# Second mixture: row loads released two experts ahead, transposes placed by a later landing, and token rows straight from the second layer for the last three experts

## Chip, cores and metric

The kernel runs on one core of one Trainium2 chip. The metric is the device time in microseconds (us); the profile also gives the span from the first to the last instruction of one execution.

## What is computed

A network of three parts, all in float32, with 1152 tokens of width 512:

```python
scores = q @ k.T / sqrt(64)                 # attention, 2 x 8 heads, 576 tokens, only the 32 largest of a row kept
x = softmax(masked scores) @ v              # 1152 x 512
P = sinkhorn(exp(x @ w_gate))               # mixture one: every token through all 8 experts
x = sum over e of P[:, e] * (relu(x @ w1[e]) @ w2[e])
expert = argmax(x @ w_gate2)                # mixture two: each token through one expert, at most 288 tokens each
out[i] = gate_w[i] * (relu(x[i] @ w1[expert]) @ w2[expert])      # w1: 512 x 1024, w2: 1024 x 512
```

Products are made in three float32r matmuls each (high x high, high x low, low x high), so each weight block and each activation is split into a high and a low part: ScalarE copies the high part, VectorE or GpSimd subtracts.

## The kernel before

**The order.** Nothing is issued in the order of the source. `job(engine, rank, cost, fn, deps, take, use, lag, more)` files a piece of work; `Order.run` is a planner that plays a clock for each engine, starts the job that can start first (the lowest rank among those that can start within 0.02 us) and writes its instructions into that engine's stream. Each engine then runs its own stream strictly in order. Dependencies given in `deps` act only in the plan; on the chip an instruction waits for the data and the buffers that it touches. A load on the SP queue is planned to have landed `lag + 2.3 + more` after its start or later, and what needs it is put into its engine's stream no sooner than that.

**Mixture two** (`mixture_two`) takes the experts in the order of their token counts, r = 0 to 7. From the code, expert r gets n = min(288, 1152/r) row slots, as S groups of P rows: r = 0 to 4 have 3 x 96, r = 5 has 2 x 116, r = 6 has 2 x 96, r = 7 has 2 x 82. For each expert:

- `gather` (L906): SP loads the expert's token rows from `disp` in DRAM into one of four row buffers (`x2`; two of them are halves of `xl`, which mixture one no longer needs), P partitions by S rows of 514 floats (512 values, the token's number, its gate weight).
- `ji` (L909): VectorE converts the token numbers to integers for the later scatter.
- `turn` (L918): TensorE transposes the rows, S transposes for each of 4 column blocks d; ScalarE (L922) and VectorE (L924) split the result into `hl` (printed as `v`). For r = 0 the columns come from another place.
- eight units f = 0 to 7: two weight blocks are loaded (L670, `ra` for layer 1, `rb` for layer 2, 3 buffers each) and split (`w0h`/`w0l` and `w1h`/`w1l` at L672 and L675; 3 and 4 pairs). Layer 1 (L939) is 12 matmuls of n columns; L686 and L688 apply the relu and split (`hh`, `hl`). Layer 2 (L951) has the weights stationary, 12 matmuls of n columns into 4 PSUM tiles `y`, which hold the output transposed.
- at the end 4 evictions (L959, L961) into `yt` (printed `yy`), 4 x S transposes back (`turn`, L967), S scalings by the gate weight (L974, L976) and S indirect scatters into `out` on GpSimd (L980).

TensorE's stream holds layer 1 of unit k+1 ahead of layer 2 of unit k. The ranks put the transposes of expert r beside units 1 to 4 of the expert before. Layer 1's output, `y`, and `hp` share 5 PSUM tiles (`psm`), given out in the order in which they are asked for: with four in `y`, one is left for layer 1.

Before the change, the load of expert r (r > 1) is released in the plan by the first layer-1 unit of expert r-1 (`begun`).

Of the kernel before, what the change touches and what calls it, by code (L numbers as in the profile page):

```python
# [162 lines left out]
def t_act(n, sbuf=False, ptr=0):  # L163
    return 0.05 + n * 0.000833 + 0.06 * sbuf + 0.09 * ptr


def t_dve(n, two=False):
    return 0.06 + n * 0.00104 + 0.08 * two
# [6 lines left out]
def t_pe(n):  # L175
    return max(0.109, n * 0.000443 + 0.0015)


class Net:
# [695 lines left out]
    def mixture_two(self):  # L875
        nc, E, DM, cap = self.nc, self.E, self.DM, self.cap
        fb = self.F // 128
        self.x2, self.i2, self.xs, self.yt, self.ob = (Pool([]) for _ in range(5))
        self.route_all()
        back, begun = [], None  # L880

        def over():
            self.xs.free += [(self.o.t["X"], x) for x in self.over]
            old = self.xt[1].rearrange("p a b -> p (a b)").bitcast(F32)
            self.x2.free += [(self.o.t["X"], old[:, i * 1542:(i + 1) * 1542].rearrange("p (s c) -> p s c", s=3))
                             for i in range(2)]
        self.job("X", 0, 0.0, over, deps=list(self.chain.values()))
        for r in range(E):
            n = min(cap, self.N // max(r, 1))
            S = -(-n // 128)  # L890
            P = -(-n // (2 * S)) * 2
            n = S * P
            x, idx, hl = self.x2.box(), self.i2.box(), self.xs.box()
            if r == 0:
                e, known = (lambda: slice(0, 1)), []
                row = lambda n=n: slice(0, n)
            else:
                e = lambda r=r: bass.ds(self.expert[r], 1)
                row = lambda r=r, n=n: bass.ds(self.expert[r] * cap, n)

                def read(r=r):
                    self.expert[r] = nc.sync.value_load(self.order_[0:1, r:r + 1], min_val=1, max_val=E - 1)
                known = [self.job("SP", -12, 0.1, read, deps=[self.sorted_])]

            def gather(x=x, row=row, P=P, S=S):
                nc.sync.dma_start(x.t[:P, :S], self.disp[row(), :].rearrange("(s p) d -> p s d", p=P))  # L906
            j = self.job("SP", -10 + 0.1 * r, 0.5, gather, deps=self.sent + [self.gate, begun if r > 1 else None] + known, take=[x],
                         lag=2.0, more=1.0)
            ji = self.job("DVE", 200 + r, 0.1, lambda x=x, idx=idx, P=P, S=S: nc.vector.tensor_copy(  # L909
                idx.t[:P, :S], x.t[:P, :S, 512]), deps=[j], take=[idx])  # L910
            turned = []
            for d in range(4):
                if r == 0:
                    p, jt = self.rows[d]
                else:
                    p = self.psa.box()

                    def turn(d=d, p=p, x=x, P=P, S=S):  # L918
                        for s in range(S):
                            self.tr(p.t[:, s * P:(s + 1) * P], x.t[:P, s, d * 128:(d + 1) * 128])  # L920
                    jt = self.job("PE", 1000 + self.unit + 13 + d, 0.11 * S, turn, deps=[j], take=[p], use=[x])
                jh = self.job("ACT", -950, t_act(n), lambda d=d, p=p, hl=hl, n=n: nc.scalar.activation(  # L922
                    hl.t[0][:, d, :n], p.t[:, :n], AF.Copy), deps=[jt], take=[hl] if d == 0 else [], use=[p, hl])
                jl = self.job("DVE", -950, t_dve(n), lambda d=d, p=p, hl=hl, n=n: nc.vector.tensor_sub(  # L924
                    hl.t[1][:, d, :n], p.t[:, :n], hl.t[0][:, d, :n].bitcast(F32)), deps=[jh], use=[p])
                turned += [jh, jl]
            y, hp, chain = [], [], {}
            yt, evicted = self.yt.box(), []
            for f in range(fb):
                k, rank = self.unit, 1000 + self.unit + 20  # L930
                self.unit += 1
                w1, w2 = self.weights(k, self.w21, self.w22, e, f, late=True, deps=known)
                while len(hp) < min(f + 2, fb):
                    hp.append(self.psm.box())
                h, p, j = self.h.box(), hp[f], None
                for m, (i, s, dep) in enumerate(((0, 0, w1[1]), (0, 1, w1[1]), (1, 0, w1[2]))):
                    def layer1(i=i, s=s, m=m, p=p, w1=w1, hl=hl, n=n):
                        for d in range(4):
                            nc.tensor.matmul(p.t[:, :n], w1[0].t[i][:, d, :], hl.t[s][:, d, :n],  # L939
                                             start=m == 0 and d == 0, stop=m == 2 and d == 3)  # L940
                    j = self.job("PE", rank - 1.5, 4 * t_pe(n), layer1, deps=turned + [dep, j],
                                 take=[p] if m == 0 else [], use=[w1[0], hl])
                begun = begun if f else j
                ready = self.parts(k, h, p, 0, n, [j], [h])
                for a in range(4):
                    if f == 0:
                        y.append(self.psm.box())

                    def layer2(a=a, f=f, h=h, w2=w2, y=y, n=n):
                        for m, (i, s) in enumerate(((0, 0), (0, 1), (1, 0))):  # L950
                            nc.tensor.matmul(y[a].t[:, :n], w2[0].t[s][:, a * 128:(a + 1) * 128], h.t[i][:, :n],  # L951
                                             start=f == 0 and m == 0, stop=f == fb - 1 and m == 2)
                    j = self.job("PE", rank, 3 * t_pe(n), layer2, deps=ready + [w2[1], w2[2], chain.get(a)],
                                 take=[y[a]] if f == 0 else [], use=[h, w2[0]])
                    chain[a] = j
                    if f == fb - 1:
                        def evict(a=a, y=y, yt=yt, n=n):
                            if a % 2:
                                nc.vector.tensor_copy(yt.t[:, a, :n], y[a].t[:, :n])  # L959
                            else:  # L960
                                nc.scalar.activation(yt.t[:, a, :n], y[a].t[:, :n], AF.Copy)  # L961
                        evicted.append(self.job("DVE" if a % 2 else "ACT", -940, t_dve(n), evict, deps=[j],
                                                take=[yt] if a == 0 else [], use=[y[a], yt]))
            for s in range(S):
                p, o = self.psa.box(), self.ob.box()

                def turn(s=s, p=p, yt=yt, P=P):  # L967
                    for a in range(4):
                        self.tr(p.t[:P, a * 128:(a + 1) * 128], yt.t[:, a, s * P:(s + 1) * P])
                j = self.job("PE", 1000 + self.unit + 21.6, 0.45, turn, deps=evicted, take=[p], use=[yt])  # L970

                def scale(s=s, p=p, o=o, x=x, P=P):
                    if s == 1:
                        nc.vector.tensor_scalar(o.t[:P], p.t[:P], x.t[:P, s, 513:514], None, op0=OP.mult)  # L974
                    else:
                        nc.scalar.activation(o.t[:P], p.t[:P], AF.Copy, scale=x.t[:P, s, 513:514])  # L976
                j = self.job("DVE" if s == 1 else "ACT", -100, 0.65, scale, deps=[j], take=[o], use=[p, x])

                def send(s=s, o=o, idx=idx, P=P):
                    i = nc.gpsimd.indirect_dma_start(  # L980
                        out=self.out, out_offset=bass.IndirectOffsetOnAxis(ap=idx.t[:P, s:s + 1], axis=0),
                        in_=o.t[:P], in_offset=None, bounds_check=self.N - 1, oob_is_err=False)
                    for x in self.outs:
                        self.tc.declare_no_dep(i.ins, x.ins, reason="other rows")
                    self.outs.append(i)
                back.append(self.job("POOL", 0, 1.0, send, deps=[j, ji] + self.zeroed, use=[o, idx], lag=3.0))
# [209 lines left out]
```

## Time and profile before

| | us |
|---|---|
| median of 3 runs (1314.46 to 1314.94) | 1314.78 |
| time of the profiled execution | 1314.3 |
| its span | 1312.5 |
| TensorE busy in it | 1260.8 (96%) |
| mixture two in it | about 1080 to 1312.5 |

"A <- B" in a row is "A is written from B". PE is TensorE's matmuls, ACT ScalarE, DVE VectorE, POOL GpSimd, SPq the queue that issues loads. "128*116 128x512" is a stationary operand of 128 by 116 and a moving one of 128 by 512. A wait is put down to what came last. Numbers are microseconds unless marked ns; `PEclk` is TensorE's granted clock as a share of full speed.

### The profile page before, as it was taken

To read this page: it belongs to the slowest core of one execution; us is meant where nothing else is said; L and a number is where in the kernel's file an instruction comes from. 1 tells how busy PE (TensorE), PEld (TensorE's weight loads), DVE (VectorE), ACT (ScalarE), POOL (GpSimd) and SP (SyncE) were. 2 spreads that over 40 slices of the span, in tenths; PEclk is the share of its full clock that TensorE was granted. 3 is DMA by queue.
4 is the path that set the end of the run, shared out by engine and by line. 5 is a ranking of instruction groups with operands and counts; after the bars stand their busy time and mean duration, and the time that the engine had idled before them with its cause. 6 is when DMAs were issued, how large, how long until landed. Compare 5 with 4: busy or idle time off the path is not lost.

```text
span 1312.5 us, 22337 instructions
## 1 busy us (share of the span) xinstructions
PE 1260.8 (96%) x7244; PEld 1085.8 (83%) x7244; DVE 963.5 (73%) x2333; ACT 765.4 (58%) x1787; POOL 363.9 (28%) x380
## 2 busy tenths in 40 slices
PE   7777999999999999999999999999999999999997
PEld 3434899988888888878888898999999979999996
DVE  7999999999999999955366676455555746665653
ACT  6857898888787777643433354444334524554643
POOL 5634677877444444430000010000000000011101
PEclk8999999999999999999999999999999999999989
DMA  4561465665233423234555465444444616665652
GB/s 113 141 225 33 118 172 164 180 181 160 86 105 102 123 76 101 67 106 127 170 171 170 136 197 170 127 124 126 128 128 122 192 34 181 198 181 169 189 166 53
DMA packets 228231, 180.90 MB, mean 138 GB/s; under 512 B 45060, under 2 KB 180228, under 8 KB 228114
## 3 DMA queue, kind: packets, MB, share of 16 engines
q1 hardware_dynamic: 224482, 174.58, 45.8%
q0 software_dynamic: 3024, 4.74, 1.1%
q8 instruction: 57, 0.93, 0.3%
q14 instruction: 60, 0.49, 0.1%
q10 hardware_dynamic: 608, 0.15, 0.1%
HBM read 159.20 MB, written 22.01 MB: 138 GB/s over the span
## 4 chain that ended last, share of the span: by engine, by line
PE 83%; DVE 7%; issue 3%; ACT 3%; DMA 2%; SPq 1%; POOL 0%; POOLq 0%; ACTq 0%; DVEq 0%
PE yp L752 30%; PE yp L728 30%; PE yp L939 5%; PE yp L951 5%; PE tp L222 5%; PE tp L621 3%; PE tp L514 3%; DVE wk L533 2%; DVE m L535 2%; DMA xl<-disp 1%; DMA x<-disp 1%; PE tp L1088 1%; DVE e L544 1%; ACT tp L542 1%; SPq L466 0%
## 5 line engine op out<-in xcount | busy, mean ns | idle before, releaser
L686 ACT ACTIVATE hh<-yp 128x256 fp32r<-128x256 f32 (+6 forms) x248 | 114.6, 462 | 241.3 <-PE yp L728 177.2
L672 ACT ACTIVATE w1h<-rb 128x512 fp32r<-128x512 f32 x248 | 156.6, 632 | 152.1 <-PE yp L752 116.3
L688 DVE SCALAR_TENSOR_TENSOR hl<-yp,hh 128x256 fp32r<-128x256 f32 (+6 forms) x248 | 128.3, 518 | 152.9 <-ACT hh L686 152.0
L752 PE MATMUL yp<-w1h,hh 128*128 128x512 f32 x552 | 223.1, 404 | 0.0
L752 PE MATMUL yp<-w1h,hl 128*128 128x512 f32 x552 | 217.0, 393 | 0.0
L752 PE MATMUL yp<-w1l,hh 128*128 128x512 f32 x552 | 216.9, 393 | 0.0
L675 DVE TENSOR_TENSOR w1l<-rb,w1h 128x512 fp32r<-128x512 f32 x160 | 110.6, 692 | 103.2 <-ACT w1h L672 102.8
L728 PE MATMUL yp<-xl,w0h 128*128 128x256 f32 (+2 forms) x768 | 167.1, 339 | 0.0
L728 PE MATMUL yp<-xh,w0h 128*128 128x256 f32 (+2 forms) x768 | 167.0, 339 | 0.0
L728 PE MATMUL yp<-xh,w0l 128*128 128x256 f32 (+2 forms) x768 | 166.9, 339 | 0.0
L672 ACT ACTIVATE w0h<-ra 128x512 fp32r<-128x512 f32 x256 | 159.9, 624 | 2.6 <-DMA ra<-in_moe_w_dram 2.6
L535 DVE MAX8 m<-wk 128x8 f32<-128x576 f32 x216 | 158.5, 744 | 0.5
L728 PEld LDWEIGHTS yp<-xh,w0h 128*128 128x128 f32 x768 | 131.3, 188 | 19.5 <-issue 0.4
L678 POOL TENSOR_TENSOR w0l<-ra,w0h 128x512 fp32r<-128x512 f32 x88 | 113.8, 1294 | 108.1 <-ACT w0h L672 103.6
L1147 POOL DMA_INDIRECT disp<-acc,idx x9 | 9.7, 1082 | 477.0 <-DVE run L1143 477.0
L728 PEld LDWEIGHTS yp<-xl,w0h 128*128 128x128 f32 x768 | 128.3, 189 | 9.5 <-issue 0.6
L728 PEld LDWEIGHTS yp<-xh,w0l 128*128 128x128 f32 x768 | 127.0, 189 | 9.4 <-issue 0.2
L678 POOL TENSOR_TENSOR w1l<-rb,w1h 128x512 fp32r<-128x512 f32 x88 | 113.9, 1294 | 61.0 <-ACT w1h L672 60.2
L752 PEld LDWEIGHTS yp<-w1h,hl 128*128 128x128 f32 x552 | 103.6, 188 | 22.7
L675 DVE TENSOR_TENSOR w0l<-ra,w0h 128x512 fp32r<-128x512 f32 x168 | 115.7, 689 | 6.2 <-ACT w0h L672 2.5
L752 PEld LDWEIGHTS yp<-w1h,hh 128*128 128x128 f32 x552 | 104.0, 188 | 17.1 <-issue 0.4
L752 PEld LDWEIGHTS yp<-w1l,hh 128*128 128x128 f32 x552 | 104.1, 189 | 14.3
(193 smaller groups left out, 2342.6 us busy)
## 6 DMA issues: line engine op xcount, KB each, us to landing
ra<-in_moe_w_dram SPq DMA_DIRECT2D x256, 256.0 KB, 2.8
rb<-in_moe_w_dram SPq DMA_DIRECT2D x256, 256.0 KB, 2.8
y<-ys SPq DMA_DIRECT2D x30, 256.0 KB, 2.1
ys<-y SPq DMA_DIRECT2D x22, 256.0 KB, 3.0
disp<-z SPq DMA_DIRECT2D x1, 4626.0 KB
qg<-in_q_dram SPq DMA_DIRECT2D x64, 64.0 KB, 2.3
vr<-in_v_dram SPq DMA_DIRECT2D x32, 128.0 KB, 2.3
yt<-y SPq DMA_DIRECT2D x10, 256.0 KB, 2.7
```

Source lines behind the costliest of these rows:

```text
L222: self.nc.tensor.transpose(out, in_, self.ident[:p, :p])
L514: nc.tensor.matmul(ps.t[:, :288], w, keys[k][0].t[:, half * 288:(half + 1) * 288], start=m == 0, stop=m == len(terms) - 1)
L535: j = self.job("DVE", r, 0.66, lambda i=i: nc.vector.max(m.t[:, i + 1], wk.t), deps=[j], use=[wk] if i == 2 else [])
L672: jh = self.job("ACT", -500 + rank, t_act(512, True), lambda r=r, w=w: nc.scalar.activation(w.t[0], r.t, AF.Copy), deps=[j], take=[w])
L675: jl = self.job("DVE", -100 + rank, t_dve(512, True), lambda r=r, w=w: nc.vector.tensor_sub(w.t[1], r.t, w.t[0].bitcast(F32)), deps=[jh], ...
L678: jl = self.job("POOL", -100 + rank, t_pool(512), lambda r=r, w=w: nc.gpsimd.tensor_sub(w.t[1], r.t, w.t[0].bitcast(F32)), deps=[jh], use=[r])
L686: jh = self.job("ACT", -1000 + k * 0.001, t_act(b - a), lambda: nc.scalar.activation(h.t[0][:, a:b], p.t[:, :b - a], AF.Relu), deps=deps, ...
L688: jl = self.job("DVE", -1000 + k * 0.001, t_dve(b - a), lambda: nc.vector.scalar_tensor_tensor(h.t[1][:, a:b], p.t[:, :b - a], 0.0, h.t[0] ...
L728: nc.tensor.matmul(p.t[:, :b - a], w1[0].t[i][:, d, :], self.xt[s][:, d, c0 + a:c0 + b], start=m == 0 and d == 0, stop=m == 2 and d == 3)
L752: nc.tensor.matmul(y[t].t, h.t[i][:, c:c + 128], w2[0].t[s], start=f == 0 and m == 0, stop=f == last and m == 2)
L939: nc.tensor.matmul(p.t[:, :n], w1[0].t[i][:, d, :], hl.t[s][:, d, :n], start=m == 0 and d == 0, stop=m == 2 and d == 3)
L951: nc.tensor.matmul(y[a].t[:, :n], w2[0].t[s][:, a * 128:(a + 1) * 128], h.t[i][:, :n], start=f == 0 and m == 0, stop=f == fb - 1 and m == 2)
```

## The change

Three edits in `mixture_two`:

1. `begun` becomes a list with one entry per expert, its layer 1 of unit f = 4; the load of expert r is released by entry r-2, that is some twelve units ahead of its own first unit where it was about eight.
2. The load's `more` goes from 1.0 to 6.5: the plan takes it as landed 5.5 us later, and puts the transposes and the number conversion later in their streams.
3. Where S is 2 (r = 5, 6, 7, `byrow`), layer 2 has the activations stationary (128 x P) and the weights moving (128 x 512): 6 matmuls of 512 columns a unit in place of 12 of n, into S PSUM tiles that hold token rows. The four evictions and the transposes back are gone; the scaling reads PSUM directly.

```diff
-        back, begun = [], None
+        back, begun = [], []
...
-            j = self.job("SP", -10 + 0.1 * r, 0.5, gather, deps=self.sent + [self.gate, begun if r > 1 else None] + known, take=[x],
-                         lag=2.0, more=1.0)
+            j = self.job("SP", -10 + 0.1 * r, 0.5, gather, deps=self.sent + [self.gate, begun[r - 2] if r > 1 else None] + known, take=[x],
+                         lag=2.0, more=6.5)
...
-            yt, evicted = self.yt.box(), []
+            byrow = S <= 2
+            yt, evicted = None if byrow else self.yt.box(), []
...
-                begun = begun if f else j
+                begun += [j] if f == 4 else []
                 ready = self.parts(k, h, p, 0, n, [j], [h])
-                for a in range(4):
+                for s in range(S if byrow else 0):
+                    if f == 0:
+                        y.append(self.psm.box())
+
+                    def rows2(s=s, f=f, h=h, w2=w2, y=y, P=P):
+                        for m, (i, t) in enumerate(((0, 0), (0, 1), (1, 0))):
+                            nc.tensor.matmul(y[s].t[:P], h.t[i][:, s * P:(s + 1) * P], w2[0].t[t],
+                                             start=f == 0 and m == 0, stop=f == fb - 1 and m == 2)
+                    chain[s] = self.job("PE", rank, 3 * t_pe(DM), rows2, deps=ready + [w2[1], w2[2], chain.get(s)],
+                                        take=[y[s]] if f == 0 else [], use=[h, w2[0]])
+                for a in range(0 if byrow else 4):
...
-                p, o = self.psa.box(), self.ob.box()
+                p, o = y[s] if byrow else self.psa.box(), self.ob.box()
...
-                j = self.job("PE", 1000 + self.unit + 21.6, 0.45, turn, deps=evicted, take=[p], use=[yt])
+                j = chain[s] if byrow else self.job("PE", 1000 + self.unit + 21.6, 0.45, turn, deps=evicted, take=[p], use=[yt])
```

## Rows read from the trace of the kernel before

**Rows 1.** The page, the chain that ended last, shares of the span by line.
```profile
PE yp L752 30%; PE yp L728 30%; PE yp L939 5%; PE yp L951 5%; PE tp L222 5%; PE tp L621 3%; PE tp L514 3%; DVE wk L533 2%; DVE m L535 2%; DMA xl<-disp 1%; DMA x<-disp 1%; PE tp L1088 1%; DVE e L544 1%; ACT tp L542 1%; SPq L466 0%
```

**Rows 2.** TensorE's waits, 1080 to 1312.5 us: total, times, longest.
```profile
PE tp L222 <- DMA xl<-disp: 3.5, 2, 2.0
PE tp L222 <- DMA x<-disp: 3.0, 1, 3.0
PE tp L1132 <- DVE hot L997: 0.9, 1, 0.9
```

**Rows 3.** Stretches: length, busy PE PEld DVE ACT POOL, PEclk, DMA share, GB/s.
```profile
1096.00:1098.00 2.00, 2.00 (x18) 2.00 (x19) 1.12 (x4) 1.42 (x4) 0.00 (x0) 1.00 1.13 324
...
1204.00:1207.00 3.00, 3.00 (x18) 3.00 (x19) 1.61 (x4) 1.48 (x3) 0.00 (x0) 0.72 0.25 87
1207.00:1210.00 3.00, 3.00 (x21) 3.00 (x19) 1.14 (x3) 0.93 (x4) 0.00 (x0) 0.71 0.66 173
...
1260.00:1264.00 4.00, 3.88 (x19) 3.88 (x20) 2.11 (x5) 1.55 (x4) 0.00 (x0) 0.50 0.47 126
1264.00:1267.00 3.00, 3.00 (x18) 3.00 (x16) 1.59 (x3) 1.12 (x3) 1.57 (x2) 0.54 0.15 55
```

**Rows 4.** The chain in order of time, 1040 to 1313 us: start, length, what.
```profile
1089.67 6.15 DMA xl<-disp
...
1194.68 9.21 DMA xl<-disp
...
1245.04 1.34 PE yp L951 x12
1246.38 1.36 PE yp L939 x12
...
1249.97 10.11 DMA x<-disp
```

**Rows 5.** Single microseconds while a row load drains (columns as in rows 3).
```profile
1205.00:1206.00 1.00, 1.00 (x8) 1.00 (x7) 0.88 (x2) 0.28 (x1) 0.00 (x0) 0.66 0.28 90
...
1261.00:1262.00 1.00, 1.00 (x7) 1.00 (x6) 0.52 (x1) 0.64 (x2) 0.00 (x0) 0.50 0.13 47
```

**Rows 6.** The page, DMA issues of the whole span: size, median us to landing.
```profile
rb<-in_moe_w_dram SPq DMA_DIRECT2D x256, 256.0 KB, 2.8
```

**Rows 7.** DMA issues between 1249 and 1262 us.
```profile
rb<-in_moe_w_dram SPq DMA_DIRECT2D x3, 256.0 KB, 9.0
```

**Rows 8.** Timelines of SP, ACT and DVE around 1096 and 1250 to 1262 us.
```profile
1250.48 0.38 SPq L670 DMA_DIRECT2D rb<-in_moe_w_dram  x1
...
1096.58 0.63 ACT L672 ACTIVATE w0h<-ra 128x512 fp32r<-128x512 f32 x1 [2.59 <-DMA ra<-in_moe_w_dram]
...
1255.83 0.33 ACT L686 ACTIVATE hh<-yp 128x192 fp32r<-128x192 f32 x1 [0.77 <-PE yp L939]
...
1260.81 0.63 ACT L672 ACTIVATE w1h<-rb 128x512 fp32r<-128x512 f32 x1 [4.13 <-DMA rb<-in_moe_w_dram]
...
1260.17 0.17 DVE L909 CAST idx<-x 82x2 int32<-82x2 f32 x1 [3.62 <-DMA x<-disp]
...
1261.48 0.69 DVE L675 TENSOR_TENSOR w1l<-rb,w1h 128x512 fp32r<-128x512 f32 x1 [0.48 <-ACT w1h L672]
```

**Rows 9.** The chain in order of time, 880 to 960 us (mixture one).
```profile
953.60 2.08 PE yp L752 x9
```

**Rows 10.** TensorE's timeline, transposes back of expert 6.
```profile
1287.63 1.04 PE L222 MATMUL tp<-ident,yy 128*96 128x128 f32 x8
1288.43 0.32 PE L951 MATMUL yp<-hh,w1h 128*128 128x164 f32 x1
```

**Rows 11.** Timeline of all engines, end of the span.
```profile
1301.76 0.28 PE L951 MATMUL yp<-hl,w1h 128*128 128x164 f32 x1
...
1302.81 0.68 ACT L976 ACTIVATE o<-tp,x 82x512 f32<-82x512 f32 x1 [0.76 <-PE tp L222]
...
1303.80 1.40 POOL L980 DMA_INDIRECT out_dram<-o,idx  x1 [11.62 <-ACT o L976]
```

## The prediction

> **What bounds the kernel now.** I read the page's chain first: layer 1 and layer 2 of both mixtures on TensorE hold it, mixture two with the lines L939 and L951, and the two row loads (x and xl from disp) have a per cent each [rows 1]. So in this stage a TensorE microsecond is a microsecond of the kernel, and what matters is where TensorE stands still. Its waits in mixture two are few: from 1082 us on three stops of 3.5 + 3.0 us, all of the transposes for a row load [rows 2]; the longest ones are 2.0 and 3.0, so the remaining one is 1.5. The chain in order of time tells which: the load of r = 1 (issued at 1089.67, 6.15 us), of r = 5 (1194.68, 9.21 us) and of r = 7 (1249.97, 10.11 us) [rows 4].
>
> The third view was the granted clock behind each stop. After the 1.5 us stop it stays at 1.00. After the 2.0 us stop it falls to the lower level (0.72 and 0.71 over two stretches of 3 us), after the 3.0 us stop it is 0.50 and then 0.54 [rows 3]. TensorE is full in these stretches, so each us at 0.5 loses half of one: 3 x 0.28 + 3 x 0.29 = 1.7 us for r = 5, 3.88 x 0.50 + 3 x 0.46 = 3.3 us for r = 7. The three stops cost 1.5, 2.0 + 1.7 = 3.7 and 3.0 + 3.3 = 6.3 us, 11.5 in all.
>
> Why are just r = 5 and r = 7 late, which load fewer rows than the others? Look at the DMA share while they drain: 0.28 with 90 GB/s at the tail of the 116-partition load, 0.13 with 47 GB/s at the tail of the 82-partition one [rows 5], that is about four and two engines of 16. The loads behind them share these engines: the three rb loads issued in that stretch landed after 9.0 us [rows 7], where 2.8 is the median [rows 6]. The Trainium skill (DMA: Bandwidth & Descriptors, "Why a DMA increments its semaphore by 16 and not by 1") states that a load runs on the largest number of engines up to 16 that divides the slowest dimension; for 96, 116 and 82 partitions that gives 16, 4 and 2. The trace agrees. The rule speaks against this change: nothing in it makes these two loads less narrow, and the second rival is what that could cost.
>
> **Edits 1 and 2, the release and the planned landing.** In the plan a row load had landed lag 2.0 + 2.3 + more 1.0 = 5.3 us after its start, now 10.8. The measured 6.15, 9.21 and 10.11 us [rows 4] lie above the first figure and below the second. Releasing behind layer 1 of unit 4 of expert r-2 leaves three units of that expert and one and a half of the next until the ranks ask for the first transposes; a unit of the narrow experts is 1.34 + 1.36 = 2.70 us [rows 4], those of 288 columns are longer, so at least 4.5 x 2.70 = 12 us pass, more than the planned 10.8. So the transposes of r = 2 to 7 no longer stop TensorE. The buffers allow it: of four, expert r takes the one of r-4, which was scaled an expert ago.
>
> For r = 5 all 3.7 us go. The weights behind it stay late (its four engines still drain it), but a unit of 288 columns is long enough that I cost this at 0, with 0 to 2 us as bounds (2.0 is its stop of today).
>
> For r = 7 the row load stops nothing any more, but what is queued behind it does. Take the stretch as it was. The rb load issued at 1250.48 reaches ScalarE only at 1260.81, which had idled 4.13 us for it [rows 8]. In ScalarE's stream the relu of the next unit stands behind that weight copy, and layer 2 of that unit waits for it. Without the stop of the transposes, TensorE would go on from 1257.1 with a layer 1, a layer 2 and a layer 1 that are ready, the last because two tiles in y in place of four leave layer 1 three PSUM tiles where it had one: 3 x 1.35 = 4.05, until 1261.15. The relu part comes at 1260.81 + 0.63 + 0.33, the VectorE part behind w1l: about 1261.5 + 0.69 + 0.36 (taken like the 0.33) = 1262.6 [rows 8]. So a stop of 1.5 us stays, moved to where the load is now issued, units 4 to 7 of r = 5. One of 1.5 us left the clock alone [rows 3], so I add nothing. Gain 6.3 - 1.5 = 4.8; bounds 0 (a stop as long as today's, with its clock) and 6.3.
>
> For r = 1 the release is as before and the later planned landing alone helps: transposes and the number conversion go 5.5 us later, past the 1.5 us stop. The two row loads at the start still delay the weights behind them: ScalarE waited 2.59 us for ra until 1096.58 [rows 8], now ahead of relus that TensorE will need. Between 0 and 1.5 us; I take 1.0. The conversion is the other cover: it stood at the head of VectorE's stream for 3.62 us at r = 7 with a weight part behind it [rows 8]; it moves later by the same 5.5 us and costs 0, and if it still came early it would only lengthen the stop just priced.
>
> The loads themselves are the same eight, in the same queue; SP has one more load in flight, and each delays the weights behind it as it did. The load of r = 2 now falls into the catching up after the first two; I cost it at 0, bounded by their 1.5 us.
>
> **Edit 3, layer 2 with tokens as output rows.** Per unit 12 matmuls of n columns took 1.34 us [rows 4]. Six of 512 columns: mixture one does nine such in 2.08 us [rows 9], 0.231 each, so 1.39. That is 0.05 us more for each of 24 units, +1.2. Only the width of the stationary operand differs from those rows (P instead of 128); no row has this form, so the bounds are 0.2 below (if a narrower weight load helps) and the first rival of the other sign above.
>
> Removed: eight transposes back at r = 5 and r = 6. Those of r = 6 take from 1287.63 to 1288.43, 0.80 us [rows 10]; those of r = 5 ran at the low clock, whose loss is counted above, so again 0.8. Together 1.6. The evictions were hidden behind TensorE; without them ACT and DVE only have less to do.
>
> At the end the last matmul ends at 1301.76 + 0.28 = 1302.04 and the first scatter starts at 1303.80, 1.76 later, with evictions, transposes and the scaling of 0.68 in between, and 0.31 from its end to the scatter [rows 11]. Now the first token group ends three matmuls (0.69 us) ahead of the second, its scaling of 0.68 runs meanwhile, and the scatter starts 0.05 - 0.69 + 0.68 + 0.31 = 0.35 us after the end. The second scatter stands behind the first on GpSimd either way. Gain 1.4; a 512-column matmul ends some 0.1 later after its start, so 1.3.
>
> **Sum.** 1.0 + 3.7 + 4.8 - 1.2 + 1.6 + 1.3 = 11.2 us. The profiled execution took 1314.3, so 1303.1. The median of the runs is 0.5 above it: 1303.6.
>
> **Rivals.**
> - *Forecast:* as summed, 1303.6; within the bounds of its terms 1301 to 1306. Chance 0.56.
> - *The stop moves to the weights behind the narrow loads.* The wait of 4.13 us for rb [rows 8] speaks for it: if ScalarE's order puts more behind the late copy than I read, TensorE stands for 2 us or more and the clock falls. Then the 4.8 us of r = 7 aren't gained: 1308.4; with the 3.7 of r = 5 too, 1312.1. The three PSUM tiles for layer 1 and the longer units at r = 3 speak against it. This is also what the skill's rule on the engines of a load would make of the change. Chance 0.25, mostly the first.
> - *The late weights are hidden altogether.* Three pairs of each weight are split ahead; if the relu comes before the late copy in ScalarE's stream, the 1.5 us go as well, and r = 1 gives its 1.5: 1301.6. Chance 0.11.
> - *Slower: the 512-column matmuls with 82 to 116 stationary columns don't run one behind the other.* Without them the change gains 12.4 us, 0.52 for each of 24 units; so from 1.34 + 0.52 = 1.86 us for six, 0.31 each, it is a loss. At twice today's 0.231 it would be 144 x 0.231 = 33 us more, 1337. The rows of 512 columns [rows 9] speak against it: nothing there depends on the stationary width. Chance 0.04.
> - *The loads go no earlier.* In SP's stream they stand between weight loads that wait for their buffers. If they stay as late as now, and the transposes too, only edit 3 is left: 1.6 + 1.3 - 1.2 = 1.7 us, 1312.9. Chance 0.04.
>
> **Numbers.** Predicted 1303.6, the forecast's time. The range runs from 1300.5 (hidden altogether, layer 2 a little cheaper, and the 0.3 that one execution may differ by) to 1309 (the moved stop at r = 7, with half a us to spare); outside are the slower case, the loads that go no earlier, and the moved stop at both experts, together some 0.15. 0.2% is 2.6 us, about what a measurement can tell from no change. Faster by more: forecast, hidden, and nearly all of the moved stop, 0.91; within: the loads that go no earlier and the worst of the moved stop, 0.05; slower 0.04.
>
> **What would show it.** In the profile after: no wait of L918's transposes for a row load among TensorE's waits at r = 5 and r = 7; the row loads of r = 2 to 7 issued about four units earlier than now in their expert order; in r = 5 (units 4 to 7) a wait of ScalarE for rb of about 3.7 us and a TensorE stop near 1.5 us on layer 2 with the clock at 1.00; layer 2 of the last three experts at 1.39 us for six; the first scatter of r = 7 about 0.35 us after the last matmul. A clock of 0.5 anywhere behind 1090 us, or a six of more than 1.5 us, would make the prediction wrong.

## The result, and the profile after

The changed kernel takes 1302.34 us (median of 4 runs, 1300.84 to 1302.58), the one before 1314.86 in the same sittings: 12.5 us less, ratio 0.9899 with a 95% interval of 0.9881 to 0.9916. Forecast were 1303.6 and a range of 1300.5 to 1309. The profiled execution took 1300.84 with a span of 1299.1, 13.4 us under the span before (it was the fastest of the four, so the spans differ by more than the medians); 0.4 of it lie before 1080 us, which the change doesn't touch (the last tile's routing ends that much earlier), 13.0 in mixture two. Layer 1 of mixture two is now line L940, layer 2 L962 with n columns and L952 with token rows, the scatter L991.

The page's chain by line, to be held against [rows 1]: the row loads are gone from it, and weight loads stand there instead.

```profile
PE yp L752 31%; PE yp L728 30%; PE yp L940 5%; PE yp L962 5%; PE tp L222 4%; PE tp L621 3%; PE tp L514 3%; DVE wk L533 2%; DVE m L535 2%; DMA rb<-in_moe_w_dram 1%; PE tp L1099 1%; DVE e L544 1%; DMA ra<-in_moe_w_dram 0%; ACT eth L581 0%; ACT tp L542 0%
```

TensorE's waits from 1080 us on, to be held against [rows 2]: 6.5 us of waiting for row loads have become 0.9 for VectorE and ScalarE. The row for ScalarE shows only the first wait of one layer 2, which in all stands still for 0.7 us, as worked out further down.

```profile
PE yp L940 <- DVE hl L688: 0.7, 1, 0.7
PE yp L952 <- ACT hh L686: 0.2, 1, 0.2
```

The granted clock where it fell before (columns as in [rows 3]): 1.00 throughout.

```profile
1200.00:1210.00 10.00, 10.00 (x81) 10.00 (x80) 6.20 (x13) 6.08 (x13) 3.08 (x3) 1.00 0.63 189
...
1240.00:1250.00 10.00, 9.77 (x60) 8.00 (x59) 5.84 (x14) 5.54 (x12) 1.48 (x2) 1.00 0.56 175
```

The place that was to keep a stop: the load of r = 7, now issued during r = 5. First SP's timeline, the chain's row for the rb load behind it, then ScalarE's and TensorE's timelines.

```profile
1232.78 0.27 SPq L906 DMA_DIRECT2D x<-disp  x1
1234.23 0.35 SPq L670 DMA_DIRECT2D rb<-in_moe_w_dram  x1
...
1234.23 10.31 DMA rb<-in_moe_w_dram
...
1244.62 0.63 ACT L672 ACTIVATE w1h<-rb 128x512 fp32r<-128x512 f32 x1 [3.67 <-DMA rb<-in_moe_w_dram]
1245.16 0.34 ACT L686 ACTIVATE hh<-yp 128x232 fp32r<-128x232 f32 x1
...
1245.56 0.49 PE L952 MATMUL yp<-w1h,hh 128*116 128x512 f32 x1 [0.17 <-ACT hh L686]
1245.88 0.40 PE L952 MATMUL yp<-w1l,hh 128*116 128x512 f32 x1
1246.34 0.49 PE L952 MATMUL yp<-w1h,hl 128*116 128x512 f32 x1
```

The rb load behind the row load still needs 10.3 us, ScalarE waits 3.67 us for it, the relu behind it starts at 1245.16, and TensorE's layer 2 begins as soon as the relu's high part is there. The end of the kernel, to be held against [rows 11]:

```profile
1289.60 0.39 PE L952 MATMUL yp<-w1h,hl 128*82 128x512 f32 x1
1290.34 1.40 POOL L991 DMA_INDIRECT out_dram<-o,idx  x1 [18.08 <-ACT o L987]
1292.04 1.41 POOL L991 DMA_INDIRECT out_dram<-o,idx  x1 [0.30 <-issue]
```

The first scatter starts 0.35 us after the last matmul's end at 1289.99; before, 1.76.

### The profile page after: what moved, and what is told of

It is laid out like the page before. It is cut to its first block, busy times and chain, and to the rows that moved or that the text cites. A ratio compares the mean times of both kernels' runs of the same rounds, so it can differ in the third digit from the quotient of the medians.

```text
span 1299.1 us, 21982 instructions
## 1 busy us (share of the span) xinstructions
PE 1252.1 (96%) x7076; PEld 1068.1 (82%) x7076; DVE 960.6 (74%) x2327; ACT 762.4 (59%) x1781; POOL 364.0 (28%) x380
## 4 chain that ended last, share of the span: by engine, by line
PE 83%; DVE 6%; issue 4%; ACT 2%; DMA 1%; POOL 0%; POOLq 0%; ACTq 0%; DVEq 0%
PE yp L752 31%; PE yp L728 30%; PE yp L940 5%; PE yp L962 5%; PE tp L222 4%; PE tp L621 3%; PE tp L514 3%; DVE wk L533 2%; DVE m L535 2%; DMA rb<-in_moe_w_dram 1%; PE tp L1099 1%; DVE e L544 1%; DMA ra<-in_moe_w_dram 0%; ACT eth L581 0%; ACT tp L542 0%
```

## Experiments

Each was timed against the kernel before on the same chip; the gain is the difference of the two medians there. Those medians of before are 1314.69 for the first four, 1314.64 for the next four, 1316.52 for the last two (three chips). The first two agree with the 1314.86 above, so times of runs 1 to 8 and of the changed kernel are compared as they are; the last is 1.9 us higher, from seven runs between 1311.77 and 1317.26.

**1. Edit 3 alone** (the changed kernel with edits 1 and 2 taken back)

```diff
-        back, begun = [], []
+        back, begun = [], None
...
-            j = self.job("SP", -10 + 0.1 * r, 0.5, gather, deps=self.sent + [self.gate, begun[r - 2] if r > 1 else None] + known, take=[x],
-                         lag=2.0, more=6.5)
+            j = self.job("SP", -10 + 0.1 * r, 0.5, gather, deps=self.sent + [self.gate, begun if r > 1 else None] + known, take=[x],
+                         lag=2.0, more=1.0)
...
-                begun += [j] if f == 4 else []
+                begun = begun if f else j
```

> Edit 3 alone: layer 2 by token rows for the last three experts, release and planned landing as before. My theory: the three stops on row loads stay as they were (1.5, 2.0 and 3.0 us, with the clock at its lower level behind the last two), and only the transposes back and the end are gained: 1.7 to 2.9 us, so about 1312. Rival (edit 3 does most of it, through the three PSUM tiles for layer 1): the stops at r = 5 and r = 7 shrink, gain of 6 us or more, 1308 or less.

1314.42 (ratio 0.9996, 0.9987 to 1.0005): no gain that can be told from none, where both theories had one. TensorE's waits in its profile (of an execution of 1316.67, the longest of its eleven, 2.3 above their median), the chain's rows for the loads of r = 5 and r = 7, the first scatter of r = 5, and the DMA queue of the scatters while the load of r = 7 drained, 1252.5 to 1266.5 us (packets, MB, share):

```profile
PE tp L222 <- DMA x<-disp: 5.8, 1, 5.8
PE tp L222 <- DMA xl<-disp: 5.2, 2, 3.3
...
1196.37 10.46 DMA xl<-disp
...
1252.92 13.02 DMA x<-disp
...
1255.15 1.27 POOL L991 DMA_INDIRECT out_dram<-o,idx  x1 [11.75 <-ACT o L987]
...
q0 software_dynamic: 512, 0.16, 5.0%
```

The first scatter of r = 5 in the kernel before:

```profile
1265.13 1.26 POOL L980 DMA_INDIRECT out_dram<-o,idx  x1 [24.54 <-ACT o L976]
```

The stop of r = 7 grew from 3.0 to 5.8 us, that of r = 5 from 2.0 to 3.3. In this execution, 2.4 us longer than the profiled one of before, the longer stops more than take back the 2 to 3 us of TensorE that edit 3 saves; how much they take in one near the median, no profile shows. Before the change no scatter ran while the load of r = 7 drained (its stretch has no row of that queue): the first one started 15.2 us after this load was issued ([rows 4], 1249.97). With token rows it starts 2.2 us after (1252.92 to 1255.15), and 512 packets run in the same stretch as the load. Run 8 tests, on the kernel of run 3, whether that slows it. The load of r = 5 took 10.46 us where it had taken 9.21, and no scatter ran beside it, so the scatters don't explain its longer stop; the cause of that stays open.

**2. Edits 1 and 2 alone** (`byrow = False`)

> Edits 1 and 2 without edit 3: layer 2 as before in all experts, one PSUM tile left for layer 1. My theory: no wait for a row load, but the late rb behind the 82-partition load now stops TensorE by one layer 1 (1.34 us) more than the 0.7 us seen with three tiles, 2 to 2.8 us and perhaps a lower clock behind it; gain 7 to 9.5 us, 1305.5 to 1308. Rival (the one tile does not matter): stop of 0.7 us as with edit 3, gain about 10.2 us, 1304.6.

1308.06 (0.9943, 0.9930 to 0.9956), a gain of 6.6, just past the end of my theory's range. One wait of layer 1 for the VectorE part of the relu, that is for its only PSUM tile (2.9; the other of the two, 1.0, is at r = 1), the chain's row for the late rb, and the clock behind it:

```profile
PE yp L940 <- DVE hl L688: 3.9, 2, 2.9
...
1235.01 10.81 DMA rb<-in_moe_w_dram
...
1250.00:1252.00 2.00, 2.00 (x11) 2.00 (x11) 1.32 (x3) 1.02 (x4) 0.00 (x0) 0.50 0.78 234
```

With three tiles the rb behind the same row load cost 0.7 us; with one 2.9 and a stretch at half the clock. About half a us of that is rb itself, which landed after 10.8 us here and 10.3 there. Edits 1 and 2 give 6.6 without edit 3 and 12.5 with it, where alone it gives nothing. Of the difference of 5.9 the shorter path is about 2.5 (the terms of layer 2, the transposes back and the end, worked out below); that the rest is the two tiles which edit 3 sets free fits the longer stop and its clock, but no run has the tiles without the token rows, so this split is argued and not shown.

**3. Edits 2 and 3, release one expert ahead as before**

> Edits 2 and 3; the release stays one expert ahead. My theory, as the planned 10.8 us are above the longest measured 10.1: the later placing alone removes the waits for row loads, and the early release is not needed; within 1 us of the changed kernel, 1301.5 to 1303.5, with the late rb costing about the same near r = 6. Rival (the release does it): transposes of r = 5 and r = 7, or the first layer 1 behind them, wait again, 3 us or more above the changed kernel.

1305.89 (0.9933, 0.9921 to 0.9945): the rival's time, by another way than it named. No transposes wait for rows; the planned landing alone did that. But ScalarE waits 6.59 us for rb behind the load of r = 7, and layer 2 stops 3.0 us with the clock down behind it (0.56 and 0.58 in the two stretches of 2 us from 1260). ScalarE's and TensorE's rows, the rb's landing, and the scatters' queue from 1246 to 1260 us:

```profile
1259.81 0.63 ACT L672 ACTIVATE w1h<-rb 128x512 fp32r<-128x512 f32 x1 [6.59 <-DMA rb<-in_moe_w_dram]
1260.71 0.74 PE L952 MATMUL yp<-w1h,hh 128*96 128x512 f32 x1 [2.97 <-ACT hh L686]
...
rb<-in_moe_w_dram SPq DMA_DIRECT2D x1, 256.0 KB, 12.7
...
q0 software_dynamic: 512, 0.16, 5.1%
```

My theory fell: with this release the load of r = 7 drains together with the scatters of r = 5, as in run 1. In the changed kernel it drains beside those of r = 4, which move as many bytes in 192 packets (1232.5 to 1246 us).

**4. Edits 1 and 3, planned landing as before**

> Edits 1 and 3; planned landing as before (more 1.0). My theory: the transposes of r = 2 to 7 are placed by their rank and find their rows; r = 1 has its 1.5 us stop again, and the number conversion stands at the head of VectorE's stream for 3 us or more behind the narrow loads and lengthens the stops at r = 5 and r = 7 to 1 to 2 us each: 1303 to 1306. Rival (the landing edit is worth r = 1 alone): no wait of VectorE's conversion above 1 us, 1303.0.

1305.47 (0.9925, 0.9912 to 0.9938), as my theory had it. TensorE's waits, and those of VectorE's number conversion:

```profile
PE tp L222 <- DMA xl<-disp: 1.6, 1, 1.6
PE yp L952 <- DVE hl L688: 1.4, 1, 1.4
PE yp L940 <- DVE hl L688: 1.4, 1, 1.4
...
DVE idx L909 <- DMA x<-disp: 5.4, 2, 4.0
DVE idx L909 <- DMA xl<-disp: 4.8, 2, 3.1
```

r = 1 has its stop again (1.6), and the conversion, put at the head of VectorE's stream too early, holds back the relu behind it at r = 5 and at r = 7 (1.4 each). Beside the other two, edit 2 is worth 3.1 us.

**5. The changed kernel with wider loads**

```diff
-            P = -(-n // (2 * S)) * 2
+            P = -(-n // (16 * S)) * 16
```

> The changed kernel with P rounded up to a multiple of 16: r = 5 loads 2 x 128 rows for 2 x 116, r = 7 2 x 96 for 2 x 82 (more row slots, same result). My theory (few engines make these loads late): the load of r = 7 drains on all engines, no wait of ScalarE for rb above 1 us behind it, its stop of 0.7 us goes; r = 5 pays some 0.3 us for 256 columns; 1301.6 to 1302.2. Rival (the place in the queue makes them late, not the width): rb still waits about 3.7 us, stop 0.7 us, 1302.5 or more as more bytes move.

1298.74 (0.9880, 0.9865 to 0.9895), 3.6 us under the changed kernel, more than either theory (the spans differ by 2.2, as the profiled execution of the changed kernel was its fastest). The only wait for a load that is left after 1085 us is that at r = 1; the load of r = 7 (385.5 KB) lands after 5.7 us:

```profile
ACT w0h L672 <- DMA ra<-in_moe_w_dram: 2.6, 1, 2.6
...
x<-disp SPq DMA_DIRECT2D x1, 385.5 KB, 5.7
```

That gives the 0.7: no wait for rb is left. The 256 columns of r = 5 cost 1.42 us a layer 1 in place of 1.34, 0.6 in all. What I had not seen is the end. Last two scatters and their queue, first with 96 rows each (this run), then the queue's row of the changed kernel, with 82:

```profile
1291.43 0.92 POOL L991 DMA_INDIRECT out_dram<-o,idx  x1 [18.15 <-ACT o L987]
1292.66 0.92 POOL L991 DMA_INDIRECT out_dram<-o,idx  x1 [0.30 <-issue]
...
q0 software_dynamic: 128, 0.06, 4.1%
```

```profile
q0 software_dynamic: 704, 0.07, 6.6%
```

With 96 partitions the scatters are 128 packets and the kernel ends 5.5 us after the first one starts (1291.43 to 1296.9); with 82 they are 704 packets and it ends 8.8 us after (1290.34 to 1299.1). That is 3.3 us. So most of this run's gain comes from the scatters, which the same line makes wider, and not from the loads.

**6. The kernel before with the same wider loads**

```diff
-            P = -(-n // (2 * S)) * 2
+            P = -(-n // (16 * S)) * 16
```

> The kernel before with the same wider loads and nothing of the change. My theory: the stops of r = 5 and r = 7 go without any earlier release, with the clock losses behind them (3.7 and 6.3 us), only r = 1 keeps its 1.5; 1304.5 to 1307. Rival (the release was too late whatever the width): these stops stay at 2 us or more each; 1312 or more.

1302.76 (0.9910, 0.9897 to 0.9924): this one line gives 11.9 us, nearly what the change gives. Both stops are gone with the release where it was; only r = 1 still waits. TensorE's wait, and the first scatter of r = 7:

```profile
PE tp L222 <- DMA xl<-disp: 1.6, 1, 1.6
...
1295.51 0.92 POOL L980 DMA_INDIRECT out_dram<-o,idx  x1 [11.63 <-ACT o L976]
```

It adds up: 3.7 + 6.3 for the stops and their clock, 3.2 at the end (first scatter to end 8.7 before, 5.5 here), less about 1.3 for 256 columns in 16 layers of r = 5. Against run 5, which has the same wide loads and the three edits, it is 4.0 us longer: with these loads the whole change is worth 4.0 us and not 12.5.

**7. Run 3 with the wider loads** (release one expert ahead, planned landing later, token rows)

> Release one expert ahead, later planned landing, token rows (the kernel of the run with edits 2 and 3), with the wider loads. If the 6.6 us that ScalarE waited for rb there came from the narrow load of r = 7 (lengthened by the scatter of r = 5 on its engines), the wait falls under 1 us and the time is that of the changed kernel with wide loads within 1 us, 1301 to 1303. Rival (the late release itself costs it): 1305 to 1306, as without the wider loads.

1298.61 (0.9876, 0.9861 to 0.9891), within 0.2 us of run 5, which releases two experts ahead. No wait for rb is left, as the theory had it; its 1301 to 1303 was missed, as in run 5, by the end that neither foresaw. With P rounded up the early release is worth nothing that these runs can tell. The wider P changes two things at once here: the load of r = 7, and the scatters of r = 5, which are 160 packets in the stretch of this load instead of 512. Run 8 takes the scatters alone.

**8. Run 3 without the scatters of r = 5**

```diff
-                back.append(self.job("POOL", 0, 1.0, send, deps=[j, ji] + self.zeroed, use=[o, idx], lag=3.0))
+                if r != 5:
+                    back.append(self.job("POOL", 0, 1.0, send, deps=[j, ji] + self.zeroed, use=[o, idx], lag=3.0))
+                else:
+                    back.append(self.job("X", 0, 0.0, lambda: None, deps=[j, ji], use=[o, idx]))
```

> Edits 2 and 3 with the release one expert ahead, narrow loads, and the two scatters of expert r = 5 left out (its token rows are not written). If the scatter made the narrow load of r = 7 slower than in the changed kernel (rb landing 12.7 us after its issue, there 10.3), rb lands after 10.5 us or less and the 3.0 us stop falls to 1.5 or less: 1302.5 to 1304. Rival (the scatter has no part): rb stays at 12 us or more, stop 3 us, 1305.9.

1302.46 (0.9906, 0.9891 to 0.9921). ScalarE's row for that rb, its landing and TensorE's wait:

```profile
1258.52 0.63 ACT L672 ACTIVATE w1h<-rb 128x512 fp32r<-128x512 f32 x1 [4.77 <-DMA rb<-in_moe_w_dram]
...
rb<-in_moe_w_dram SPq DMA_DIRECT2D x1, 256.0 KB, 10.9
...
PE yp L952 <- ACT hh L686: 1.1, 1, 1.1
```

The landing falls from 12.7 to 10.9 us, the stop from 3.0 to 1.1, the time by 3.4 us, near that of the changed kernel. The landing lies between theory and rival (10.5 or less, 12 or more), stop and time are the theory's. SP issues the row load and the four loads behind it at the same distances in both runs, so it is the scatters of r = 5 that made the late release cost something.

**9. Run 5 with the row load of r = 0 released later**

```diff
-        self.x2, self.i2, self.xs, self.yt, self.ob = (Pool([]) for _ in range(5))
+        self.x2, self.i2, self.xs, self.yt, self.ob = (Pool([], n > 0) for n in range(5))
...
+            if r:
+                j, ji = load(begun[r - 2] if r > 1 else None)
...
+                if r == 0 and f == 2:
+                    ji = load(j)[1]
```

`load(after)`, whose lines are left out here, files the gather and the number conversion as before, released by `after`. The first edit lets the row buffers be given out in the order in which their loads start.

> The changed kernel with wide loads, and the row load of r = 0, which only the scaling at the end of its units needs, released by layer 1 of unit 2 in place of standing ahead of all. My theory: the stop of 0.7 us left at r = 1 comes from weights that land behind two row loads of 578 KB; with one of them ScalarE's wait for ra (2.6 us) falls under 1 us and the stop goes, 0.5 to 0.9 us less than with wide loads alone: 1297.8 to 1298.3. Rival (the weights are late because the queue stood in the expert reads before): wait and stop stay, 1298.7.

1298.44 (0.9873, 0.9850 to 0.9895), 0.3 under run 5 and inside the spread of either (and beside a kernel before that is 1.9 longer). In SP's timeline the load of r = 0 (now xl) is issued only 1.5 us behind that of r = 1, with two weight loads ahead of it. ScalarE's waits go from 2.6 for ra to 2.1 for ra and 2.4 for rb, and the stop moves to the transposes of r = 1, which now wait for VectorE:

```profile
1090.36 0.36 SPq L906 DMA_DIRECT2D x<-disp  x1
1090.83 0.95 SPq L670 DMA_DIRECT2D ra<-in_moe_w_dram  x2
1091.87 0.46 SPq L906 DMA_DIRECT2D xl<-disp  x1
...
PE tp L222 <- DVE v L928: 1.1, 1, 1.1
```

Neither theory is decided: the load hardly moved on the chip, since SP reaches both only at 1090 us.

**10. Run 9 with 2 x 120 rows for r = 5**

```diff
-            P = -(-n // (16 * S)) * 16
+            P = 120 if r == 5 else -(-n // (16 * S)) * 16
```

> As the run before, with 2 x 120 rows for r = 5 in place of 2 x 128. 15 engines should drain it by the rule that a load takes the largest number up to 16 that divides its partitions, so no wait behind it; layer 1 of r = 5 goes from 1.42 back to about 1.36 us: 0.4 to 0.6 us less than the run before. Rival (only a multiple of 16 spreads the load): a stop or a wait of 1 us or more at r = 5, no gain or a loss.

1297.68 (0.9870, 0.9847 to 0.9892), the lowest median here, 0.8 under run 9. The executions of the two runs overlap (1296.63 to 1298.81, 1297.17 to 1299.48), so the times alone don't settle it. The load of r = 5 lands after 5.3 us (after 5.1 with 128 rows in run 9) and layer 1 takes 1.34. The chain's rows for the first layer 1 of r = 5 and of r = 6, here and then in run 9:

```profile
x<-disp SPq DMA_DIRECT2D x1, 481.9 KB, 5.3
...
1220.35 1.34 PE yp L944 x12
...
1244.49 1.32 PE yp L944 x12
```

```profile
1221.27 1.42 PE yp L944 x12
...
1246.00 1.32 PE yp L944 x12
```

The units of r = 5 take 24.1 us here and 24.7 in run 9: the 0.6 that was expected. The rest of the 0.8 lies elsewhere.

## Why the prediction was right, step by step

- **Where TensorE stood still, and what it cost.** Shown: 3.7 us for r = 5 and 6.3 for r = 7 with the clock behind them. Run 6 takes these two stops away by another means, and its gain adds up with them and the shorter end.
- **Transposes find their rows after edits 1 and 2.** Right: no wait for a row load in the profile after. Which of the two does it was left together in the prediction; runs 3 and 4 part them. The later planned landing is enough for the transposes. The early release moves the load of r = 7 away from the scatters of r = 5, which edit 3 brings forward: 3.6 us (run 3 against the changed kernel).
- **The weights behind the narrow load still come late.** Right in mechanism and in the wait: about 3.7 us forecast, 3.67 measured. The prediction doesn't say how it came to 3.7, so that it met the number this closely proves little, and may be luck. The size of what stays was off: 1.5 us forecast, 0.7 measured (layer 2 of that unit ends 2.11 us after layer 1 in place of 1.39, 1245.25 to 1247.36). The step that was mis-sized had layer 2 wait for the VectorE part; it starts with the ScalarE part and needs the other only at its third matmul, 1246.34. The kernel's order of these matmuls says so, and the two ahead of it are worth about 0.5 of the 0.8; the other 0.3 is that TensorE's ready work lasted until 0.6 us after the weight copy began (1244.62 to 1245.25), where 0.3 had been worked out.
- **r = 5 pays nothing for its late weights, r = 1 keeps part.** Right: no stop at r = 5, where ScalarE waited 1.5 us for rb (the row below, less the 3.67); r = 1 went from 1.5 to 0.7, a gain of 0.8 for 1.0.

```profile
ACT w1h L672 <- DMA rb<-in_moe_w_dram: 5.2, 2, 3.7
```

- **Three PSUM tiles for layer 1 cover the late weights.** Run 2 agrees: with one tile 2.9 us and half the clock, for an rb that came 0.5 us later.
- **Layer 2 with 512 columns.** Six took 1.38 to 1.41 us for 1.39 forecast, with 82, 96 and 116 stationary columns. (The rows of mixture one that the prediction held against its slower rival all have 128 and could not speak on the width; these do.) Layer 1 between them went from 1.34 to about 1.31, so that a whole unit with 82 rows stays at 2.68 us, as the two starts of layer 1 show. Instead of +1.2 it costs about 0.5 in 24 units.

```profile
1283.09 1.02 PE L940 MATMUL yp<-v,w0h 128*128 128x164 f32 x8
...
1285.77 1.02 PE L940 MATMUL yp<-v,w0h 128*128 128x164 f32 x8
```

- **Transposes back and the end.** The end gave 1.4 (0.35 us to the first scatter, both forecast and measured). The 1.6 is taken as worked out: the eight transposes are gone, and no row measures the term by itself. That the rest of the end, 8.8 us, hangs on 82 rows in a scatter was not seen.
- **The loads go earlier.** Right: those of r = 2 to 7 are issued 13 to 19 us earlier, four to five units and up to 5 us by which TensorE itself is ahead. The rival that had them stay as late gave 1312.9; 1.7 us under 1314.8 is 1313.1.

The terms now give 0.8 + 3.7 + 5.6 - 0.5 + 1.6 + 1.4 = 12.6 of 13.0 us in the spans of the two profiled executions; 0.4 is not accounted for. The sum had 11.2; the 1.3 us between the forecast and the median are mostly the stop at r = 7 and layer 2.

The terms don't stand for the edits one by one. Edit 3 alone gives nothing, edits 1 and 2 without it 6.6, all three 12.5: what one sets free the next late load takes, until no row load is waited for.

The cause under the stops is the width of two loads, as far as these runs go: with P rounded up, both stops of the kernel before go and nothing of the release is changed, 8.7 of the 11.9 us of run 6 (3.7 + 6.3 less the 1.3 for 256 columns). The other 3.2 there, and most of the 3.6 in run 5, are the last scatters. The Trainium skill (DMA: Bandwidth & Descriptors, "Why a DMA increments its semaphore by 16 and not by 1") has a load run on the largest number of engines up to 16 that divides the slowest dimension of its source and of its destination. The traces agree for 116 and 82 partitions (4 and 2 engines; DMA shares of 0.28 and 0.13 at their tails, [rows 5]). For 120 partitions it gives 15; the 5.3 us to landing, about the 5.1 of 128, fit many engines and don't count them.

## What to carry to other kernels

When a load lands late, look at how many engines drain it before you move it: a row count that divides badly was worth 12 us of 1314 here (8.7 by the loads, 3.2 by the last scatters), was mended in one line, and delayed the loads behind it wherever these runs issued it. With that line in, all three edits together were worth 4.0 us. A load or a helper instruction that is put too early in an in-order stream stops what stands behind it, so price the plan's landing by the slowest measured one. And free PSUM tiles count as slack: a weight block that landed after 10.3 us cost 0.7 us with three of them, one that landed after 10.8 cost 2.9 with one.

## What the runs showed of the hardware that was not expected

- At the kernel's end an indirect scatter of 82 partitions took 1.40 us on GpSimd and 352 packets (704 for two), one of 96 partitions 0.92 us and 64 packets; the end came 3.3 us sooner with the wider one. Amid other work scatters of 96 partitions took 0.91 to 1.34 us.
- Scatters slow a narrow load that drains at the same time: rb behind it landed after 12.7 us with 512 packets of scatters in the stretch (run 3), after 10.9 without (run 8), and after 10.3 in the changed kernel with 192 packets of as many bytes (0.16 MB).
- Twelve matmuls of layer 1 take 1.31 to 1.36 us with 164, 192, 232 or 240 columns, 1.42 or 1.43 with 256 and 1.56 to 1.61 with 288, at full clock and without a stop. Padding r = 7 from 82 to 96 rows a group cost layer 1 nothing that these rows show, while r = 5 paid for 128 and not for 120.
